# VectorE's convolution lane moved from two units ahead to one, and the second block's dense convolution cut to one group

## The chip, the cores and the metric

The kernel runs on one core of a Trainium2 chip. The metric is the device time of one launch in microseconds (us); of the runs shown, the median counts. TensorE (PE in the profile) does the matmuls, VectorE (DVE), ScalarE (ACT) and GpSimd (POOL) the elementwise work, and SyncE (SP) issues transfers. Each has its own queue of instructions. Matmul results go to PSUM, which here is handed out in four tiles of two banks each.

## The reference

A causal convolution over 7 tokens, whose weights are a softmax per head (8 heads of 24 columns), is followed by a gated feed-forward layer with ReLU. There are 8 batches of 4096 tokens and 192 columns; the hidden width is 1536.

```python
w = np.exp(weight - np.max(weight, axis=-1, keepdims=True))
w = w / (np.sum(w, axis=-1, keepdims=True) + 1e-09)
x_pad = np.concatenate([np.zeros((B, pad, D)), x], axis=1)
idx = np.arange(S)[:, None] + np.arange(K)[None, :]
x_unf = x_pad[:, idx, :].reshape(B, S, K, H, group)
a = np.einsum('hk,bskhg->bshg', w, x_unf).reshape(B * S, D)
gate = np.maximum(a @ w_gate, 0.0)
val = a @ w_val
return gate * val @ w_out
```

## The kernel before

**Units and streams.** The work is cut into 16 units of 1024 tokens (`UNIT`). Each is done for two streams at once (`st`): batch b and batch b + 4. The convolved input of a unit is the tile `xc[u]`: partitions 0 to 63 hold one stream and 64 to 127 the other, with the 192 columns in three chunks (`c`), and the tokens run along the free dimension.

**The main loop** (lines 648 to 685) does for each unit u: the gates (`gate_val`, twice, for 512 tokens each), then the projection (`project`). In `gate_val`, each of 12 steps f makes 12 matmuls (line 505) into two PSUM tiles, one for the gate and one for the value; ScalarE takes the ReLU of the first (line 516), VectorE multiplies it by the second (line 517) into `hT`. A PSUM tile is free again when its reader is done.

**The projection** multiplies `hT` by `Wo` for four halves (512 tokens of one stream each). In units 1 to 15 `half_pass` does it with matmuls of 64 rows (line 536), in two turns for a half, the turns of different halves interleaved: (0,0), (1,0), (0,1), (2,0), (1,1), (3,0), (2,1), (3,1), as (half, turn). The second turn of a half writes the same banks from other rows, so it must wait for the first turn to end. That wait goes by way of SyncE: an empty instruction in SyncE's queue (line 549) waits for the last matmul of the first turn, and the first matmul of the second turn waits for it (line 546). In unit 0 `half_whole` does it with full 128-row matmuls (line 556) and no such wait. `evict` (line 573) copies a half's result to SBUF, and SyncE issues the write to DRAM (line 574).

**The convolution** has two ways.

- *Dense, on TensorE*, for units 0 and 1. `GROUPS` lists four groups of five token pieces. Groups 0 and 1 make unit 0: `conv_dense`, one call for each chunk of columns (line 333), with one PSUM tile each. Group 0 stands before the gates, and the three calls of group 1 stand in unit 0's first gates, ahead of f = 5, 7 and 9. Groups 2 and 3 make unit 1: `conv(g, part)`, eight matmuls (line 358) in two parts with one PSUM tile each. ScalarE moves the results in five copies to a tile `y` (line 373), and SyncE issues one transposing transfer for each token piece from `y` into `xc[1]` (line 395). Group 2 stands after unit 0's gates, group 3 after the first half of its projection.
- *The lane*, for units 2 to 15, two units ahead: while unit u runs, the lane makes unit u + 2. GpSimd issues four loads of x into `x_e` (`lane_load`, line 414), copies them into another order in `x_p` (line 433), and SyncE issues nine transposing transfers (line 436) into `x_r`. The first 576 tokens (`LDVE`) are VectorE's: ScalarE makes the first products (`lane_first`, line 469), VectorE adds 18 shifted products (`lane_rest`, line 481). The other 448 tokens (`LPOOL`) are GpSimd's: ScalarE (line 452) and VectorE (line 454, the list `VECTOR`) make products into `prods`, and GpSimd adds them (line 458) during the gates of the next unit.

**Order.** The schedule is manual: each engine's queue holds its instructions in the order in which the program text makes them. After unit u's gates come `lane_first` and `lane_rest` of unit u + 2 and then `project(u)`, in which ScalarE's products and the copies of the results alternate.

**The head.** GpSimd loads the gate and value weights in column pieces (`load_w`) into partitions 0 to 63, and `both_halves` copies each piece into partitions 64 to 127: VectorE does pieces 0 and 1, GpSimd (`pool_halves`, line 180) the others. Piece 3 serves f = 5 and 6, piece 4 f = 7 and 8, piece 5 f = 9 to 11. After these copies GpSimd issues the loads for lane 2 and for groups 2 and 3 and the load of `Wo`.

Of the kernel before, what the change touches and what calls it, by code (L numbers as in the profile page):

```python
# [15 lines left out]
def kernel(  # L16
# [26 lines left out]
    VECTOR = [  # L43
        [(0, 5), (1, 5), (2, 5), (0, 4), (1, 4), (2, 4), (2, 1)],
        [(0, 5), (1, 5), (2, 5), (0, 6), (2, 1)],
    ]
# [11 lines left out]
    second = [min(t, 2 * UNIT - SUB) for t in range(UNIT, 2 * UNIT, SUB)]  # L58
    GROUPS += [(0, second[:GSUB]), (0, second[GSUB:])]
# [3 lines left out]
    xpool = ctx.enter_context(tc.tile_pool(name="xpool", bufs=3))  # L63
# [3 lines left out]
    ypool = ctx.enter_context(tc.tile_pool(name="ypool", bufs=2))  # L67
# [7 lines left out]
    def load_x(g):  # L75


        bp, toks = GROUPS[g]
        xt = xpool.tile([128, GSUB, 2, D], F16, name="x_h")
        rows, step = (SUB, DSUB) if g < 2 else (128, SUB)  # L80
        for st in range(2):
            b = bp + NB * st
            last = toks[-1] - toks[-2] != step
            n_full = len(toks) - int(last)
            src = bass.AP(
                tensor=x.tensor,
                offset=x.offset + (b * S + toks[0] - PAD) * D,
                ap=[[D, rows], [step * D, n_full], [1, D]],
            )
            nc.gpsimd.dma_start(out=xt[0:rows, 0:n_full, st, :], in_=src)  # L90
            if last:
                nc.gpsimd.dma_start(
                    out=xt[0 : SUB + PAD, len(toks) - 1, st, :],
                    in_=x[b, toks[-1] - PAD : toks[-1] + SUB, :],
                )
        return xt

# [87 lines left out]

    load_w(0)
# [5 lines left out]
    load_w(4, 6)  # L192
    pool_halves(3)

# [150 lines left out]
    convs = {}  # L345

    def conv(g, part):


        xt = xts[g]  # L350
        bp, toks = GROUPS[g]
        n = len(toks)
        rows = SUB + PAD
        W = 2 * n * G
        ps = psum.tile([128, 2, 512], FP, name="ps")
        for h, (t, bank, slot) in PLACE.items():
            if t == part:
                nc.tensor.matmul(  # L358
                    out=ps[0:SUB, bank, W * slot : W * (slot + 1)],
                    lhsT=band(h),  # L360
                    rhs=xt[0:rows, 0:n, :, G * h : G * (h + 1)],
                    start=True,
                    stop=True,
                    skip_group_check=True,
                )
        if part == 0:
            convs[g] = ypool.tile([128, GSUB, NCH, 2, 64], F16, name="y")
        y = convs[g]

        def move(copy, bank, i0, step_in, c, r0, step_out, width):  # L370
            src = ps[0:SUB, bank, 0 : 2 * W]
            dst = y[0:SUB, 0:n, 0, :, 0:1]
            copy(
                out=bass.AP(
                    tensor=dst.tensor,
                    offset=dst.offset + 128 * c + r0,
                    ap=[dst.ap[0], [step_out, 2], [NCH * 128, n], [64, 2], [1, width]],
                ),
                in_=bass.AP(
                    tensor=src.tensor,  # L380
                    offset=src.offset + i0,
                    ap=[src.ap[0], [W + step_in, 2], [2 * G, n], [G, 2], [1, width]],
                ),
            )

        if part == 0:
            move(nc.scalar.copy, 0, 0, 0, 0, 0, G, G)
            move(nc.scalar.copy, 1, 0, 0, 1, 8, G, G)
            return
        move(nc.scalar.copy, 0, 0, 0, 2, 16, G, G)  # L390
        move(nc.scalar.copy, 1, 0, 8, 0, 48, 2 * 128 - 48, 16)
        move(nc.scalar.copy, 1, 16, -16, 1, 0, 56, 8)
# [7 lines left out]
    xes, xrs, accs, prods = {}, {}, {}, {}  # L400

    def lane_load(u):


        bp, t0 = u * UNIT // S, u * UNIT % S
        xe = epool.tile([128, TILES, 2, NCH, 64], F16, name="x_e")
        j0 = int(t0 == 0)
        if j0:
            nc.gpsimd.memset(xe[0:HALO, 0, :, :, :], 0.0)
        for st in range(2):  # L410
            b = bp + NB * st
            for j, n in ((j0, TDVE - j0), (TDVE, TILES - TDVE)):
                lo = t0 - HALO + 128 * j if j < TDVE else t0 + LDVE - HALO
                nc.gpsimd.dma_start(  # L414
                    out=xe[:, j : j + n, st, :, :].rearrange("p j c r -> p j (c r)"),
                    in_=bass.AP(
                        tensor=x.tensor,
                        offset=x.offset + (b * S + lo) * D,
                        ap=[[D, 128], [128 * D, n], [1, D]],
                    ),  # L420
                )
            if j0:
                nc.gpsimd.dma_start(
                    out=xe[HALO:128, 0, st, :, :].rearrange("p c r -> p (c r)"),
                    in_=x[b, 0 : 128 - HALO, :],
                )
        xes[u] = xe

    def lane_turn(u):
        xe = xes.pop(u)  # L430
        xp = epool.tile([128, TILES, NCH, 2, 64], F16, name="x_p")
        for st in range(2):
            nc.gpsimd.tensor_copy(out=xp[:, :, :, st, :], in_=xe[:, :, st, :, :])  # L433
        xr = rpool.tile([128, NCH, 128 * TILES], F16, name="x_r")
        for j in range(TILES):
            nc.sync.dma_start_transpose(
                out=xr[:, :, 128 * j : 128 * j + 128],
                in_=xp[:, j].rearrange("p c s r -> p (c s r)"),
            )
        xrs[u] = xr  # L440

    def shifted(u, c, k, lane):
        o = HALO - KW + 1 + k
        if lane:
            return xrs[u][:, c, 128 * TDVE + o : 128 * TDVE + o + LPOOL]
        return xrs[u][:, c, o : o + LDVE]

    def product(engine, u, c, k):
        out = prods[u][:, k, c, :]
        in_, scale = shifted(u, c, k, 1), tap[:, c, k : k + 1]  # L450
# [5 lines left out]
    def add(u, k):  # L456
        pr = prods[u]
        nc.gpsimd.tensor_tensor(  # L458
            out=pr[:, 0] if k < KW - 1 else xc[u][:, :, LDVE:UNIT],
# [5 lines left out]
    def lane_first(u):  # L465
        accs[u] = apool.tile([128, NCH, LDVE], FP, name="acc")
        xc[u] = xcpool.tile([128, NCH, UNIT], F16, name="xc")
        for c in range(NCH):
            nc.scalar.activation(  # L469
                out=accs[u][:, c, :],  # L470
                in_=shifted(u, c, 0, 0),
# [3 lines left out]
        prods[u] = apool.tile([128, KW, NCH, LPOOL], FP, name="prods")  # L475

    def lane_rest(u):
        acc = accs.pop(u)
        for k in range(1, KW):
            for c in range(NCH):  # L480
                nc.vector.scalar_tensor_tensor(  # L481
                    out=xc[u][:, c, 0:LDVE] if k == KW - 1 else acc[:, c, :],
                    in0=shifted(u, c, k, 0),
# [5 lines left out]
        for c, k in VECTOR[u > 2]:  # L489
            product(nc.vector, u, c, k)  # L490

    def gate_val(u, w):
        h = hpool.tile([128, NFF, 2, WIN], F16, name="hT")
        xcb = xc[u]
        for f in range(NFF):
            if u == 0 and w == 0 and f in (5, 7, 9):
                conv_dense(1, (f - 5) // 2)
# [28 lines left out]
    SYNC = mybir.DependencyInfo(mybir.DependencyClass.Sync, mybir.DependencyReason.DATA)  # L526

# [24 lines left out]

    def half_whole(h, st, outs):
        for q in range(4):
            for f in range(NFF):
                nc.tensor.matmul(  # L556
                    out=outs[q],
                    lhsT=h[:, f, st, 128 * q : 128 * (q + 1)],
                    rhs=Wo[:, f, :],
                    start=(f == 0),  # L560
                    stop=(f == NFF - 1),
                )
# [45 lines left out]
    def project(u, hs, work):  # L608
# [3 lines left out]
        if u == 0:  # L612
            order = [(i, 2) for i in range(4)]
        if u == NUNIT - 1:
            order = [(0, 0), (1, 0), (0, 1), (2, 0), (1, 1), (2, 1), (3, 2)]
        for i, turn in order:
# [5 lines left out]
            if turn in (0, 2):  # L622
                at[i] = slots()
            if turn in (1, 2):
                for c, k in work[i]:
                    product(nc.scalar, u + 2, c, k)
            if turn == 2:
                half_whole(h, st, at[i][1])
            else:
                done[i] = half_pass(h, st, at[i][1], turn, done.get(i))  # L630
            if turn:
                evict(at[i][0], row0, u > 0 and i == 3 or u == NUNIT - 1 and i == 2)
            if u == 0 and i == 0:
                conv(3, 0)
                conv(3, 1)
# [7 lines left out]
    pool_halves(5)  # L643
    nc.gpsimd.tensor_copy(out=tap[64:128], in_=tap[0:64])
    lane_load(2)
    xts[2] = load_x(2)
    nc.gpsimd.dma_start(out=Wo[:], in_=moe_w_out.rearrange("(c p) d -> p c d", p=128))
    for u in range(NUNIT):
        lane = 1 <= u < NUNIT - 1
        if lane:  # L650
            add(u + 1, 1)
        if u == 1:
            lane_load(3)
            add(2, 2)
            add(2, 3)
# [3 lines left out]
        if u + 2 < NUNIT:  # L659
            lane_turn(u + 2)  # L660
        if u == 0:
            xts[3] = load_x(3)
# [53 lines left out]
```

## Time and profile before

| what | value |
|---|---|
| median of 3 runs | 768.06 us (767.74 to 768.5) |
| the profiled execution's own time | 767.88 us |
| its span in the profile | 765.9 us |
| ReLU, line 516 | 386 times, mean 1019 ns |
| gate product, line 517 | 386 times, mean 1215 ns |
| product and sum on VectorE, line 481 | 210 + 42 times, mean 811 and 810 ns |
| product on ScalarE, line 452 | 222 times, mean 662 ns |
| product on VectorE, line 454 | 72 times, mean 446 ns |
| addition on GpSimd, line 458 | 70 + 14 times, mean 3034 and 3027 ns |
| transposing transfer, line 395 | 10 times, 1174 / 1246 / 1814 ns (least, median, most) |
| transposing transfer, line 436 | 126 times, 1180 / 1257 / 3183 ns |
| load of x_e, line 414, issue to landing | 4.2 / 6.1 / 9.5 us |
| empty instruction, line 549 | 59 times, 17 ns each |

How to read it: the page gives the busy time of each engine and its share of the span. The chain that ended last is followed back from the last instruction, at each step to what released it; "PE ps L505" is TensorE's work of line 505 into the tile `ps`. Lines of a timeline have start, length, engine, line, operation, output<-inputs, shape and count; a bracket gives the idle time before and what ended it. "SPq" and "POOL DMA" lines are the issuing of transfers, not the moving of the data. The gaps between instructions of one engine can be smaller than the durations suggest, since the next one starts before the end of the last is reported.

### The profile page before, as it was taken

To read this page: it belongs to the slowest core of one execution; us is meant where nothing else is said; L and a number is where in the kernel's file an instruction comes from. 1 tells how busy PE (TensorE), PEld (TensorE's weight loads), DVE (VectorE), ACT (ScalarE), POOL (GpSimd) and SP (SyncE) were. 2 spreads that over 40 slices of the span, in tenths; PEclk is the share of its full clock that TensorE was granted. 3 is DMA by queue.
4 is the path that set the end of the run, shared out by engine and by line. 5 is a ranking of instruction groups with operands and counts; after the bars stand their busy time and mean duration, and the time that the engine had idled before them with its cause. 6 is when DMAs were issued, how large, how long until landed. Compare 5 with 4: busy or idle time off the path is not lost.

```text
span 765.9 us, 24782 instructions
## 1 busy us (share of the span) xinstructions
PE 761.7 (99%) x10794; PEld 502.5 (66%) x10794; DVE 692.7 (90%) x746; ACT 600.7 (78%) x735; POOL 369.9 (48%) x212
## 2 busy tenths in 40 slices
PE   9999999999999999999999999999999999999998
PEld 4595674946749476584755848567484674947648
DVE  7999999999999999999999999999999999996591
ACT  6797887878878787887878878788787887875571
POOL 8608648093570926619166290743908346090000
PEclk9999999999999999999999999999999999999999
DMA  8966727190472804528054281722919131200202
GB/s 121 134 104 116 92 91 88 54 122 6 100 78 66 110 23 97 61 85 95 23 111 47 85 92 44 106 31 85 93 44 117 21 92 39 65 22 15 71 2 84
DMA packets 131810, 56.12 MB, mean 73 GB/s; under 512 B 96741, under 2 KB 131701, under 8 KB 131701
## 3 DMA queue, kind: packets, MB, share of 16 engines
q1 hardware_dynamic: 90789, 38.85, 25.1%
q0 software_dynamic: 40768, 15.59, 18.9%
q8 instruction: 84, 1.38, 0.8%
q14 instruction: 25, 0.20, 0.1%
q10 hardware_dynamic: 144, 0.10, 0.0%
HBM read 31.68 MB, written 25.17 MB: 74 GB/s over the span
## 4 chain that ended last, share of the span: by engine, by line
PE 99%; DMA 1%; issue 0%; POOL 0%; ACT 0%; POOLq 0%
PE ps L505 65%; PE ps L536 31%; PE ps L556 2%; DMA x_h<-in_x_dram 1%; PE ps L594 1%; PE ps L333 0%; PE ps L358 0%; POOL spaced L129 0%; ACT acc L573 0%; POOLq L700 0%
## 5 line engine op out<-in xcount | busy, mean ns | idle before, releaser
L517 DVE TENSOR_TENSOR hT<-gr,ps 128x1024 f16<-128x1024 f16 (+1 forms) x386 | 468.9, 1215 | 37.0 <-ACT gr L516 9.9
L516 ACT ACTIVATE gr<-ps 128x1024 f16<-128x1024 f32 (+1 forms) x386 | 392.9, 1019 | 102.4 <-PE ps L505 100.6
L458 POOL TENSOR_TENSOR prods<-prods 128x1344 f32<-128x1344 f32 x70 | 212.4, 3034 | 309.1 <-DVE prods L454 305.7
L505 PE MATMUL ps<-xc,Wg 64*128 64x512 f16 x2304 | 311.9, 376 | 0.0
L505 PE MATMUL ps<-xc,Wv 64*128 64x512 f16 x2304 | 311.8, 376 | 0.0
L536 PEld LDWEIGHTS <-hT 64*128 64x128 f16 x5664 | 234.1, 94 | 3.6
L536 PE MATMUL ps<-Wo,hT 64*128 64x192 f16 x5664 | 236.1, 243 | 0.0
L505 PEld LDWEIGHTS <-Wv 64*128 64x128 f16 x2304 | 129.8, 94 | 118.5 <-DVE hT L517 0.3
L505 PEld LDWEIGHTS <-Wg 64*128 64x128 f16 x2304 | 112.2, 94 | 132.4 <-issue 0.2
L481 DVE SCALAR_TENSOR_TENSOR acc<-x_r,tap,acc 128x576 f32<-128x576 f16 x210 | 154.3, 811 | 1.6 <-ACT acc L469 1.6
L452 ACT ACTIVATE prods<-x_r,tap 128x448 f32<-128x448 f16 x222 | 130.3, 662 | 0.0
L573 ACT COPY out_s<-ps 128x768 f32<-128x768 f32 (+1 forms) x63 | 45.7, 725 | 52.4 <-PE ps L536 42.5
L414 POOL DMA_DIRECT2D x_e<-in_x_dram x56 | 45.1, 818 | 3.4 <-POOL x_p L433 3.4
L433 POOL COPY x_p<-x_e 128x1728 f16<-128x1728 f16 x28 | 44.7, 1624 | 1.7 <-DMA x_e<-in_x_dram 1.6
L458 POOL TENSOR_TENSOR xc<-prods 128x1344 f16<-128x1344 f32 x14 | 42.4, 3027 | 1.1
L481 DVE SCALAR_TENSOR_TENSOR xc<-x_r,tap,acc 128x576 f16<-128x576 f16 x42 | 31.8, 810 | 0.0
L573 DVE COPY out_s<-ps 128x384 f32<-128x384 f32 x15 | 8.3, 550 | 25.5 <-ACT out_s L573 25.5
L469 ACT ACTIVATE acc<-x_r,tap 128x576 f32<-128x576 f16 x42 | 29.4, 766 | 0.0
L454 DVE TENSOR_SCALAR prods<-x_r,tap 128x448 f32<-128x448 f16 x72 | 27.3, 446 | 0.0
L556 PE MATMUL ps<-Wo,hT 128*128 128x192 f16 x192 | 16.2, 246 | 0.0
L556 PEld LDWEIGHTS <-hT 128*128 128x128 f16 x192 | 15.9, 98 | 0.0
L90 POOL DMA_DIRECT2D x_h<-in_x_dram x6 | 4.9, 825 | 0.0
(54 smaller groups left out, 66.9 us busy)
## 6 DMA issues: line engine op xcount, KB each, us to landing
out_dram<-out_s SPq DMA_DIRECT2D x63, 384.0 KB
x_e<-in_x_dram POOLq DMA_DIRECT2D x34, 192.0 KB, 6.2
x_e<-in_x_dram POOLq DMA_DIRECT2D x22, 240.0 KB, 4.8
x_r<-x_p SPq DMA_TRANSPOSE x126
Wo<-in_moe_w_out_dram POOLq DMA_DIRECT2D x1, 576.0 KB
x_h<-in_x_dram POOLq DMA_DIRECT2D x2, 240.0 KB, 7.6
x_h<-in_x_dram POOLq DMA_DIRECT2D x2, 210.0 KB, 5.1
x_h<-in_x_dram POOLq DMA_DIRECT2D x2, 192.0 KB, 7.6
```

The source lines that it names most:

```text
L414: nc.gpsimd.dma_start(out=xe[:, j : j + n, st, :, :].rearrange("p j c r -> p j (c r)"), in_=bass.AP(tensor=x.tensor, offset=x.offset + (b ...
L433: nc.gpsimd.tensor_copy(out=xp[:, :, :, st, :], in_=xe[:, :, st, :, :])
L452: engine.activation(out=out, in_=in_, func=ACTF.Copy, scale=scale)
L458: nc.gpsimd.tensor_tensor(out=pr[:, 0] if k < KW - 1 else xc[u][:, :, LDVE:UNIT], in0=pr[:, 0], in1=pr[:, k], op=ALU.add,)
L469: nc.scalar.activation(out=accs[u][:, c, :], in_=shifted(u, c, 0, 0), func=ACTF.Copy, scale=tap[:, c, 0:1],)
L481: nc.vector.scalar_tensor_tensor(out=xc[u][:, c, 0:LDVE] if k == KW - 1 else acc[:, c, :], in0=shifted(u, c, k, 0), scalar=tap[:, c, k : k ...
L505: nc.tensor.matmul(out=pss[i][:, st, :], lhsT=W[64 * st : 64 * st + 64, c, 128 * f : 128 * (f + 1)], rhs=xcb[64 * st : 64 * st + 64, c, WI ...
L516: nc.scalar.activation(out=gr[:, sts], in_=pss[0][:, sts], func=ACTF.Relu)
L517: nc.vector.tensor_tensor(out=h[:, f, sts], in0=gr[:, sts], in1=pss[1][:, sts], op=ALU.mult)
L536: mm = nc.tensor.matmul(out=outs[q], lhsT=h[64 * r : 64 * r + 64, f, st, 128 * q : 128 * (q + 1)], rhs=Wo[64 * r : 64 * r + 64, f, :], sta ...
L556: nc.tensor.matmul(out=outs[q], lhsT=h[:, f, st, 128 * q : 128 * (q + 1)], rhs=Wo[:, f, :], start=(f == 0), stop=(f == NFF - 1),)
L573: one(out=dst[:, step * j : step * j + step], in_=src[:, step * j : step * j + step])
```

## The change

VectorE's part of the lane is now made one unit ahead and GpSimd's part two units ahead. Lane v (v = 1 to 15) makes the first 576 tokens of unit v and the last 448 tokens of unit v + 1; `pieces(v)` gives the two pieces of x. While unit u runs, lane u + 1 is made. Lane 15 has no GpSimd part.

- Of unit 1, only the last 448 tokens are convolved on TensorE: one group of four pieces, `GROUPS[2]`, in place of groups 2 and 3. `conv` fills two PSUM tiles at once, and `conv_out` holds ScalarE's five moves and SyncE's transposing transfers. `conv` stands after unit 0's gates, and `lane_first(1)` now stands between it and `conv_out`.
- The three calls of `conv_dense` for group 1 stand together ahead of f = 6.
- `half_whole` is gone: unit 0's projection uses `half_pass` in the same order as the other units, and its last result is split between ScalarE and VectorE as theirs are.
- Lane 1's x is loaded at the head, through the generator `lane_load`: two loads ahead of `pool_halves(3)`, one behind it, the last after `pool_halves(5)`. Its turn comes in two halves, with the load of `Wo` and of group 2 between them. Lane 2's load is held until `lane_first(1)` is done (`hold`).
- `lane_turn` makes four copies of parts in place of two of the whole.
- `VECTOR` is one list of five products; before, unit 2's lane had seven. In lane 1, GpSimd makes two products itself (`FOR_POOL`). All of a lane's additions on GpSimd now stand ahead of the unit's gates in the program text.
- `xpool` has two buffers in place of three, `ypool` one in place of two.

```diff
-    VECTOR = [
-        [(0, 5), (1, 5), (2, 5), (0, 4), (1, 4), (2, 4), (2, 1)],
-        [(0, 5), (1, 5), (2, 5), (0, 6), (2, 1)],
-    ]
+    VECTOR = [(0, 5), (1, 5), (2, 5), (0, 6), (2, 1)]
+    FOR_POOL = [(1, 6), (2, 6)]
...
-    second = [min(t, 2 * UNIT - SUB) for t in range(UNIT, 2 * UNIT, SUB)]
-    GROUPS += [(0, second[:GSUB]), (0, second[GSUB:])]
+    GROUPS += [(0, list(range(UNIT + LDVE, 2 * UNIT, SUB)))]
...
+    def pieces(v):
+        both = [(0, TDVE, v * UNIT)]
+        if v + 1 < NUNIT:
+            both.append((TDVE, TILES - TDVE, (v + 1) * UNIT + LDVE))
+        return both
+
+    def lane_load(v, hold=None):
...
+                if hold is not None:
+                    tc.add_manual_dep(first.ins, hold.ins.name, SYNC, reason="behind the turns of the lane before")
+                    hold = None
...
+    ahead = lane_load(1)
+    next(ahead)
+    next(ahead)
     pool_halves(3)
+    next(ahead)
...
-    def conv(g, part):
+    def conv(g):
...
+        wide = [psum.tile([128, 2, 512], FP, name="ps") for _ in range(2)]
+        for h, (t, bank, slot) in PLACE.items():
+            nc.tensor.matmul(
+                out=wide[t][0:SUB, bank, W * slot : W * (slot + 1)],
...
+        return wide
+
+    def conv_out(g, wide):
...
+        y = ypool.tile([128, GSUB, NCH, 2, 64], F16, name="y")
...
+        move(nc.scalar.copy, 0, 0, 0, 0, 0, 0, G, G)
+        move(nc.scalar.copy, 0, 1, 0, 0, 1, 8, G, G)
+        move(nc.scalar.copy, 1, 0, 0, 0, 2, 16, G, G)
+        move(nc.scalar.copy, 1, 1, 0, 8, 0, 48, 2 * 128 - 48, 16)
+        move(nc.scalar.copy, 1, 1, 16, -16, 1, 0, 56, 8)
         for jj, t in enumerate(toks):
             u, k = t // UNIT, min(SUB, UNIT - t % UNIT)
             nc.sync.dma_start_transpose(
...
+    def lane_turn(v):
...
+        for j0, n, _ in pieces(v):
+            for st in range(2):
+                nc.gpsimd.tensor_copy(
+                    out=xp[:, j0 : j0 + n, :, st, :], in_=xe[:, j0 : j0 + n, st, :, :]
                 )
+            for j in range(j0, j0 + n):
+                nc.sync.dma_start_transpose(
...
-            if u == 0 and w == 0 and f in (5, 7, 9):
-                conv_dense(1, (f - 5) // 2)
+            if u == 0 and w == 0 and f == 6:
+                for c in range(NCH):
+                    conv_dense(1, c)
...
-        if u == 0:
-            order = [(i, 2) for i in range(4)]
...
-                evict(at[i][0], row0, u > 0 and i == 3 or u == NUNIT - 1 and i == 2)
-            if u == 0 and i == 0:
-                conv(3, 0)
-                conv(3, 1)
+                evict(at[i][0], row0, i == 3 or u == NUNIT - 1 and i == 2)
...
     pool_halves(4)
     pool_halves(5)
+    load_rest(ahead)
     nc.gpsimd.tensor_copy(out=tap[64:128], in_=tap[0:64])
-    lane_load(2)
+    between = lane_turn(1)
+    next(between)
+    nc.gpsimd.dma_start(out=Wo[:], in_=moe_w_out.rearrange("(c p) d -> p c d", p=128))
     xts[2] = load_x(2)
-    nc.gpsimd.dma_start(out=Wo[:], in_=moe_w_out.rearrange("(c p) d -> p c d", p=128))
+    load_rest(between)
     for u in range(NUNIT):
...
+        adds = 1 <= u < NUNIT - 1
+        if u + 1 < NUNIT:
+            xc[u + 1] = xcpool.tile([128, NCH, UNIT], F16, name="xc")
+        if adds:
+            add(u, 1)
         hs = []
         if u == 0:
             hs.append(gate_val(0, 0))
...
+        if 0 < u < NUNIT - 1:
+            load_rest(lane_turn(u + 1))
+        if 0 < u < NUNIT - 2:
+            load_rest(lane_load(u + 2))
+        if u == 1:
+            for c, k in FOR_POOL:
+                product(nc.gpsimd, u, c, k)
+        if adds:
+            for k in range(2, KW):
+                add(u, k)
         while len(hs) < 2:
             hs.append(gate_val(u, len(hs)))
...
+        wide = conv(2) if u == 0 else None
+        if u + 1 < NUNIT:
+            last = lane_first(u + 1)
+            if u == 0:
+                conv_out(2, wide)
+                load_rest(lane_load(2, last))
+            lane_rest(u + 1)
         if u + 2 < NUNIT:
...
         project(u, hs, work)
```

## The prediction

> **What bounds the kernel now.** I read the page first (busy shares, the chain that ended last), then that chain in order of time, then the timeline of each engine around the places that the change touches.
>
> ```profile
> PE 761.7 (99%) x10794; PEld 502.5 (66%) x10794; DVE 692.7 (90%) x746; ACT 600.7 (78%) x735; POOL 369.9 (48%) x212
> PE 99%; DMA 1%; issue 0%; POOL 0%; ACT 0%; POOLq 0%
> ```
>
> TensorE is the chain. A gain must take matmuls, or a wait, out of its row, and any new wait in that row is paid in full. The chain in order of time shows the stretch that the change rewrites, and then one ordinary unit:
>
> ```profile
> 21.57 19.56 PE ps L505 x180
> 41.13 0.99 PE ps L358 x8
> 42.12 3.96 PE ps L556 x48
> 46.09 0.82 PE ps L358 x8
> 46.91 11.88 PE ps L556 x144
> 58.79 31.19 PE ps L505 x288
> 89.97 15.84 PE ps L536 x384
> ```
>
> Unit 0's gates end at 41.13 and unit 1's start at 58.79: 17.66 us, in which two dense convolutions (0.99 and 0.82) stand among 15.84 of whole projections. A later unit takes 46.92 us (31.08 gates, 15.84 projection), with no hole.
>
> **What leaves TensorE's row.** Of the two groups only group 2 stays, now of 4 pieces instead of 5 (192 columns a matmul, not 240). Its second tile is still the one that VectorE frees with the last but one gate product (about 41.5), so I take 0.95 for it, between 0.8 x 0.99 = 0.8 and 0.99. The 192 whole matmuls become 384 half ones; 48 + 144 of the former took 15.84, 384 of the latter take 15.84: nothing. So 17.66 becomes 0.95 + 15.84 = 16.79: **-0.9**, if nothing waits.
>
> Group 1's three pieces (40 matmuls, 0.56 each) move together ahead of f = 6. Around each one the 24 gate matmuls take 2.70 where 288 in 31.08 make 2.59, so 0.11 a switch, and two switches go: **-0.2**. They take three of the four PSUM tiles, so f = 6 begins with the tile that VectorE's product of f = 5 frees. I work that out as 17.95, against 17.87 for TensorE: **+0.1**.
>
> **What is moved in GpSimd's queue at the head.** Two of lane 1's loads now stand ahead of the copy of the weights' upper halves for f = 5.
>
> ```profile
> 11.54 0.63 POOL L173 DMA_DIRECT2D Wv<-in_moe_w_val_dram  x1
> 13.17 0.82 POOL L180 COPY Wg<-Wg 64x768 f16<-64x768 f16 x1 [1.01 <-DMA Wg<-in_moe_w_gate_dram]
> 13.94 0.83 POOL L180 COPY Wv<-Wv 64x768 f16<-64x768 f16 x1
> 19.72 3.30 POOL L414 DMA_DIRECT2D x_e<-in_x_dram  x4
> ```
>
> Four such issues take 3.30, so two take 1.63: from 12.18 to 13.81. The wait of 1.01 hides part; the Wg copy ends near 14.63 instead of 13.99, Wv near 15.41. Before, a dense piece filled 14.41 to 14.98; now f = 5 wants its upper half at 14.43 and 15.37. With 0.1 for the signal that is 0.30 + 0.14: **+0.4**; bounds 0 (signal and copy earlier) and 0.9. The third load puts the halves for f = 7 at 17.9 and the last at 20.2, against wants of 19.2 and 21.8: nothing. Lane 1's copies then start at 21.2, its nine transposes at about 1.4 us (12.87 for nine) end near 36, and ScalarE asks for them at 41.4.
>
> **The new wait: SyncE's queue in unit 0.** Half passes come in two turns. The second turn of a half waits for an empty SyncE instruction (line 549) that waits for the first turn. Unit 0 used none before: the 59 in the trace are four in each later unit, less one. Now it has four, and in SyncE's queue they stand behind conv_out's four transposes, which wait for ScalarE's five moves, which now stand behind lane_first.
>
> ```profile
> 40.52 1.02 ACT L516 ACTIVATE gr<-ps 128x1024 f16<-128x1024 f32 x1 [0.27 <-PE ps L505]
> 41.71 2.00 ACT L373 CAST y<-ps 112x480 f16<-112x480 f32 x5 [0.17 <-PE ps L358]
> 43.57 2.14 ACT L469 ACTIVATE acc<-x_r,tap 128x576 f32<-128x576 f16 x3
> 47.82 0.81 ACT L573 COPY out_s<-ps 128x768 f32<-128x768 f32 x1
> 43.74 6.92 SPq L395 DMA_TRANSPOSE xc<-y  x5
> 50.76 0.53 SPq L574 DMA_DIRECT2D out_dram<-out_s  x1
> 51.39 8.21 SPq L395 DMA_TRANSPOSE xc<-y  x5
> 59.71 1.86 SPq L574 DMA_DIRECT2D out_dram<-out_s  x3
> ```
>
> The last four lines show what a queue behind transposes costs: the first output is in SBUF at 48.63, and its write starts at 50.76, right after the fifth transpose. Two more outputs are copied by 56.4 and their writes start at 59.71, after the next five.
>
> The new order from these rows: ReLU from 40.52, lane_first from 41.44 (0.92 later, as 370.89 to 371.81 in the seventh projection) to 43.53, moves from 43.45. Five moves of 1920 elements took 2.00; 384 fewer at 0.83 ns (1024 elements in 1.02 us against 384 in 0.48) leave 1.68: y complete at 45.13. The transposes start 0.03 later. Single ones run 1.17 to 1.81 us, median 1.25; the first four of group 2 took from 43.74 to 49.40 with the gaps, 5.66, and four median ones would take 5.2. I take 5.5: SyncE is free at 50.7, TensorE has its signal at 50.85. It wants it after conv and two half passes: 41.02 + 0.95 + 3.96 = 45.9. **TensorE stands idle for 4.9 us.** Bounds: 4.5 with the median ones; 6.7 if each takes the longest of group 2, 1.81, since lane 2's x now loads in this stretch. What is next in that queue (the write of the first output, the later turns' signals) comes due only after TensorE has moved on, at intervals of 2 us, so one stall and not four.
>
> [...]
>
> **What is hidden.** Lane 1 adds 18 products-and-sums (13.2 us, as 373.08 to 386.30) to VectorE's total, but they take lane 2's old place in unit 0; what is really added is lane 15 in unit 14's projection, where VectorE sat idle for 14.77 us. Uncovered, it would be 13 us. The price of one unit less lead is a deadline: xc must be ready when the next unit's gates start.
>
> ```profile
> 384.03 2.27 DVE L481 SCALAR_TENSOR_TENSOR xc<-x_r,tap,acc 128x576 f16<-128x576 f16 x3
> 387.17 0.81 PE L505 MATMUL ps<-xc,Wg 64*128 64x512 f16 x6
> ```
>
> It ends at 386.30 and is wanted at 387.17: 0.87 to spare, within 0.02 at all thirteen such boundaries, so nothing. In unit 0 the stall itself gives more. GpSimd's two products in unit 1 are not shown: between the 0.45 us of VectorE's product and the 3.03 of an addition of three times the elements. I take 1.0, nearest to a third of the addition. Even at 3.03 each its additions end near 89, and the buffer is overwritten from about 96. Four x_p copies for two add at most 2 x 0.2 (the smallest copy) to a queue that idles 21.7 us a unit. The load of lane 2, held to 43.5, lands by 46.8 + 9.5 = 56.3, and is copied after 61. Unit 0's last output, now split between ScalarE and VectorE, is as in every other unit.
>
> **Sum.** -0.9 - 0.2 + 0.1 + 0.4 + 4.9 = +4.3. The profiled execution took 767.88 (765.9 of span and 1.98 around it), 0.18 below the median of 768.06; 772.2 and 772.4, so **772.3**. From unit 1 on nothing changes.
>
> **The rivals.** *Forecast*, chance 0.48: 772.3, own range 771.3 to 774.1 by the bounds.
>
> *The idle stretch slows the matmuls after it*, 0.30. The trace's only matmuls after a long idle are the first:
>
> ```profile
> 0.86 2.83 PE L157 MATMUL ps<-const-bfloat16-1.0 128*128 128x512 bf16 x7 [0.86 <-PEq L700]
> ```
>
> 3200 columns in 2.83 us are 1.13 a ns, against 288 x 512 / 2 in 31.08, 2.37 a ns, later. A 512 wide one takes 0.61 still at 4.09 and 0.38 at 5.15, so the slow stretch is 3.2 to 4.3 long and costs half of itself, 1.8: 774.1. Against it: no idle of this length follows matmuls anywhere in this trace, and the granted clock shows full speed throughout. [...]
>
> *SyncE does not hold TensorE*, 0.10: the place is the first second turn, at 45.9; it decides if the four transposes leave the queue within 0.75 us, 0.19 each, where the rows have 1.25, or if the signal goes ahead of them. Then -0.9 - 0.2 + 0.1 + 0.4 = -0.6: 767.5, not slower.
>
> *VectorE misses the deadline*, 0.06: at all 15 boundaries TensorE pays what exceeds 0.87; 0.3 over would add 4.5, 776.8. For it: one late row would do it fifteen times. Against it: the same rows at thirteen boundaries. The last 0.06 is for what I have not seen.
>
> **Range and chances.** 770.8 to 775.3 holds the first two cases; the third, the fourth and the remainder leave out under 2 in 10. No change means within 0.2% (1.5 us), about what a measurement of this kernel can tell. Slower: 0.48 + 0.30 + 0.06 and 0.02 of the rest, 0.86. Within: 0.08 of the third and 0.01, 0.09. Faster: 0.02 and 0.03, 0.05.
>
> **What would show it.** In the profile after: one hole of about 5 us in TensorE's row, after the first 96 half matmuls of unit 0's projection, released by SyncE; in SyncE's queue four transposes from about 45 and the first empty instruction near 51; unit 1's gates near 63; from there 46.92 a unit. Half-rate matmuls after the hole speak for the second case, no hole for the third, a hole at each unit's first gate with VectorE as releaser for the fourth. The f = 5 gates should show 0.4 of waiting on GpSimd. I am wrong if the time is below 770, or if the hole has another releaser.

## The result

The changed kernel takes 775.65 us (median of 5, 775.48 to 775.69), the kernel before 768.39 in the same comparison: ratio 1.0096, 95% interval 1.0081 to 1.0111. It is 7.3 us slower, where 4.3 were forecast, and 0.35 above the range. The profiled execution took 775.69, with a span of 773.7. In the table of experiments, one of e10's twelve executions took 1345.67 us at a granted clock of 0.655; its ratio leaves that one out.

First the page after the change: busy times, and the chain that ended last, by engine and by line.

```profile
PE 763.9 (99%) x10978; PEld 500.5 (65%) x10978; DVE 705.6 (91%) x763; ACT 600.9 (78%) x733; POOL 377.3 (49%) x242
PEclk9989999999999999999999999999999999999999
PE 96%; POOL 1%; DMA 1%; SPq 1%; issue 1%; ACT 0%; POOLq 0%; ACTq 0%
```

TensorE is busy for 2.2 us more than before although a dense group is gone, the chain has 4% outside of it, and the granted clock, always 9 before, has an 8 in the third slice (38 to 58 us). The chain in order of time, from unit 0's gates on:

```profile
19.04 1.16 POOL Wv L171
20.20 0.65 issue
20.85 21.59 PE ps L517 x198
...
45.48 1.58 ACT y L410 x5
47.07 1.18 SPq L430
48.29 1.25 SPq L430
49.58 1.31 SPq L430
50.94 1.25 SPq L430
...
52.31 14.33 PE ps L546 x288
66.64 31.08 PE ps L517 x288
97.72 15.84 PE ps L546 x353
```

The four transposes are on the chain, and the six half passes behind them take 14.33 us where eight take 15.84 in unit 1. Another piece reads differently: "issue" at 20.20 is time in which TensorE waited for nothing that the profile shows. The chain puts a copy that ended at 20.20 ahead of it; e6 below shows that TensorE did not need that copy. From TensorE's starts in the timelines:

| stage | before | after | difference |
|---|---|---|---|
| start to unit 0's first gate | 7.80 | 8.16 | +0.36 |
| first gate to the projection's first matmul | 34.16 | 35.76 | +1.60 |
| projection to unit 1's first gate | 16.76 | 22.55 | +5.79 |
| unit 1's first gate to the end | 707.15 | 707.21 | +0.06 |

Everything happens in the first 67 us. Of the +5.79, one dense group less gives -0.9 (16.76 holds 0.9 for group 3); the idle stretch and slow matmuls make the rest. In the timeline (start, length, idle before and what ended it):

```profile
42.46 1.02 ACT L528 ACTIVATE gr<-ps 128x1024 f16<-128x1024 f32 x1 [0.27 <-PE ps L517]
43.38 2.10 ACT L478 ACTIVATE acc<-x_r,tap 128x576 f32<-128x576 f16 x3
43.92 4.13 PE L546 MATMUL ps<-Wo,hT 64*128 64x192 f16 x96
45.38 1.67 ACT L410 CAST y<-ps 112x384 f16<-112x384 f32 x5
47.07 5.12 SPq L430 DMA_TRANSPOSE xc<-y  x4
52.31 14.33 PE L546 MATMUL ps<-Wo,hT 64*128 64x192 f16 x288 [4.25 <-SPq L559]
66.47 0.81 PE L517 MATMUL ps<-xc,Wg 64*128 64x512 f16 x6
```

ReLU, lane_first, moves, transposes, signal: each starts as the one before it ends, and TensorE starts 4.4 us after the 47.88 (43.92 + 3.96) at which it could have. From 52.31 to 66.47 it needs 14.16 for six half passes, against 6/8 of 15.84 = 11.88: 2.3 lost. The table by stretches shows why; its columns are the stretch, its length, busy time of PE, PEld, DVE, ACT and POOL (with the number of instructions), granted clock, share of the DMA engines, GB/s. The share adds up the times of all packets, so it can be above 1.

```profile
44.00:47.90 3.90, 3.90 (x96) 3.82 (x96) 3.90 (x6) 3.90 (x10) 1.88 (x3) 1.00 0.14 7
47.90:52.30 4.40, 0.15 (x4) 0.00 (x0) 4.40 (x7) 1.94 (x4) 1.31 (x2) 0.76 1.33 156
52.30:54.00 1.70, 1.69 (x22) 1.59 (x24) 1.70 (x3) 0.00 (x0) 0.00 (x0) 0.50 1.54 167
54.00:56.00 2.00, 2.00 (x30) 1.86 (x28) 2.00 (x4) 0.00 (x0) 0.00 (x0) 0.50 0.77 125
56.00:58.00 2.00, 2.00 (x42) 1.93 (x38) 2.00 (x4) 1.63 (x3) 0.00 (x0) 0.74 0.03 8
58.00:60.00 2.00, 2.00 (x54) 2.00 (x50) 1.68 (x5) 1.97 (x4) 0.17 (x1) 1.00 0.65 197
```

The clock falls to 0.50 at 50.22, during the idle stretch, and stays there until 57.04 by the profile's clock record: 4.7 us of matmuls at half rate lose 2.4, near the 2.3 measured. The +1.60 ahead of the projection is mostly a hole ahead of f = 7:

```profile
17.18 0.84 POOL L171 COPY Wv<-Wv 64x768 f16<-64x768 f16 x1
18.84 0.83 PE L517 MATMUL ps<-xc,Wv 64*128 64x512 f16 x6
20.85 0.33 PEld L517 LDWEIGHTS <-Wg 64*128 64x128 f16 x6 [1.68 <-issue]
```

f = 7 should start 0.645 after 18.84, at 19.49; it starts at 20.85, 1.4 late. Its weights, piece 4, were copied by 18.02; the copies of piece 5 behind them ended at 20.20.

### The profile page after: what moved, and what is told of

It reads as the page before. It is cut to its first block, busy times and chain, and to the rows that moved or that the text cites. A ratio compares the mean times of both kernels' runs of the same rounds, so it can differ in the third digit from the quotient of the medians.

```text
span 773.7 us, 25194 instructions
## 1 busy us (share of the span) xinstructions
PE 763.9 (99%) x10978; PEld 500.5 (65%) x10978; DVE 705.6 (91%) x763; ACT 600.9 (78%) x733; POOL 377.3 (49%) x242
## 4 chain that ended last, share of the span: by engine, by line
PE 96%; POOL 1%; DMA 1%; SPq 1%; issue 1%; ACT 0%; POOLq 0%; ACTq 0%
PE ps L517 63%; PE ps L546 32%; DMA Wg<-in_moe_w_gate_dram 1%; SPq L430 1%; PE ps L593 1%; POOL Wg L171 0%; POOL Wv L171 0%; POOL Wv L164 0%; POOL Wg L164 0%; POOL x_h L84 0%; ACT y L410 0%; ACT acc L478 0%; POOL x_e L197 0%; POOL spaced L122 0%; POOL spaced L120 0%
## 5 line engine op out<-in xcount | busy, mean ns | idle before, releaser
L546 PE MATMUL ps<-Wo,hT 64*128 64x192 f16 x6048 | 254.5, 244 | 4.3 <-SPq L559 4.3
L546 PEld LDWEIGHTS <-hT 64*128 64x128 f16 x6048 | 251.7, 95 | 8.5 <-SPq L559 4.5
L490 DVE SCALAR_TENSOR_TENSOR acc<-x_r,tap,acc 128x576 f32<-128x576 f16 x225 | 165.3, 812 | 0.0
L197 POOL DMA_DIRECT2D x_e<-in_x_dram x58 | 46.9, 817 | 22.2 <-ACT acc L478 18.9
L442 POOL COPY x_p<-x_e 128x960 f16<-128x960 f16 (+1 forms) x58 | 50.4, 910 | 0.1
L490 DVE SCALAR_TENSOR_TENSOR xc<-x_r,tap,acc 128x576 f16<-128x576 f16 x45 | 34.1, 812 | 0.0
L478 ACT ACTIVATE acc<-x_r,tap 128x576 f32<-128x576 f16 x45 | 31.4, 764 | 0.0
L148 PE MATMUL ps<-const-bfloat16-1.0 128*128 128x512 bf16 (+1 forms) x10 | 4.2, 560 | 0.9 <-PEq L691 0.9
L380 ACT CAST xc<-ps 128x512 f16<-128x512 f32 x4 | 2.3, 586 | 2.4 <-PE ps L370 2.4
L593 PE MATMUL ps<-Wo,hT 128*128 128x192 f16 x48 | 4.1, 246 | 0.0
```

Of the source, the lines that this page charges most:

```text
L197: first = nc.gpsimd.dma_start(out=xe[:, j0 + start : j0 + n, st, :, :].rearrange("p j c r -> p j (c r)"), in_=bass.AP(tensor=x.tensor, off ...
L442: nc.gpsimd.tensor_copy(out=xp[:, j0 : j0 + n, :, st, :], in_=xe[:, j0 : j0 + n, st, :, :])
L478: last = nc.scalar.activation(out=accs[v][:, c, :], in_=shifted(v, c, 0, 0), func=ACTF.Copy, scale=tap[:, c, 0:1],)
L490: nc.vector.scalar_tensor_tensor(out=xc[v][:, c, 0:LDVE] if k == KW - 1 else acc[:, c, :], in0=shifted(v, c, k, 0), scalar=tap[:, c, k : k ...
L546: mm = nc.tensor.matmul(out=outs[q], lhsT=h[64 * r : 64 * r + 64, f, st, 128 * q : 128 * (q + 1)], rhs=Wo[64 * r : 64 * r + 64, f, :], sta ...
```

## The experiments

They compare the three losses: the idle stretch (4.4), the slow matmuls (2.3), the hole (1.4). Since the head differs between executions (first gate from 7.42 to 8.91 over fourteen profiles, with the same instructions ahead of it), the verdicts rest on the stages within each profile.

| run | first gate to projection | projection to unit 1 | median, us | ratio to before (interval) |
|---|---|---|---|---|
| before, and once more | 34.16, 34.29 | 16.76, 16.76 | 768.0 to 768.4; once more, one run: 767.72 | |
| after | 35.76 | 22.55 | 775.65 | 1.0096 (1.0081 to 1.0111) |
| e1 signals first | 36.79 | 16.91 | 770.69 | 1.0035 (1.0021 to 1.0048) |
| e2 wait filled | 37.25 | 20.53 | 774.16 | 1.0073 (1.0060 to 1.0086) |
| e3 moves first | 37.33 | 20.54 | 775.10 | 1.0087 (1.0070 to 1.0105) |
| e4 whole matmuls | 35.71 | 15.94 | 769.50 | 1.0014 (1.0005 to 1.0023) |
| e5 pieces spread | 34.83 | 23.11 | 773.77 | 1.0082 (1.0068 to 1.0096) |
| e6 loads late | 34.88 | 22.73 | 774.56 | 1.0086 (1.0073 to 1.0099) |
| e7 = e1 and e5 | 34.26 | 16.17 | 768.07 | 0.9999 (0.9990 to 1.0007) |
| e9 = e4 and e5 | 34.63 | 15.94 | 767.16 | 0.9989 (0.9980 to 0.9997) |
| e10 = e9, loads late | 34.13 | 15.93 | 767.46 | 0.9995 (0.9986 to 1.0004) |
| e11 = e7, no hold | 34.25 | 15.85 | 767.42 | 0.9991 (0.9982 to 0.9999) |
| e12 short idle | 38.74 | 19.51 | 774.92 (one run) | |

**e1: the signals ahead of the transposes.** The lane's part of unit 0 is written behind the first two half passes:

```diff
+            if n == 2 and between is not None:
+                between()
...
-        project(u, hs, work)
+        project(u, hs, work, lane_part if u == 0 else None)
```

> Only the order of unit 0 is changed: its first two half passes are written ahead of the lane's part, so the two empty SyncE instructions stand ahead of the four transposes. Theory (the signals wait behind the transposes, and the idle stretch lowers the matmul clock): the idle 4.43 and the slow 2.28 both go, 775.65 - 6.7 = 768.9. Rival A (TensorE waits for the transposes' data or for ScalarE's moves, not for the queue): the idle stays, 775.6. Rival B (the slow half passes come from the x loads and transposes that run at the same time, not from the idle): only the idle goes, 771.2 with half passes still slow after 52.

The idle stretch and the slow matmuls are both gone: 16.91 from projection to gates instead of 22.55, with the transposes still running from 48.75 to 53.86. So SyncE's order made the wait, not the transposes' data nor ScalarE. Rival A falls, and rival B too, since x's packets are in the same stretch (DMA share 1.57 and 1.61 from 50 to 54, at a granted clock of 1.00). The 1.8 us by which 770.69 misses 768.9 are the head of these executions (36.79, of which f = 5 takes more than in after) and a new hole of 0.88 in the projection, both taken up below.

```profile
44.45 12.55 PE L546 MATMUL ps<-Wo,hT 64*128 64x192 f16 x299
57.88 3.71 PE L546 MATMUL ps<-Wo,hT 64*128 64x192 f16 x85 [0.88 <-issue]
```

**e2: the wait filled.** The order of after, with TensorE kept busy while it waits:

```diff
+            if u == 0 and (i, turn) == (0, 1):
+                for _ in range(76):
+                    nc.tensor.matmul(
+                        out=at[1][0][:, 1, 2 * D : 512],
+                        lhsT=busy[:, 0:128],
+                        rhs=busy[:, 0:128],
...
```

> 76 matmuls of 128 columns, whose results nobody reads, fill TensorE's wait in unit 0's projection; the wait itself stays. Theory (idle lowers the clock): no slow stretch, 775.65 - 2.28 = 773.4, and the granted clock is 1.00 from 48 to 58. Rival B (transfers slow the matmuls): the half passes after the wait stay slow, 775.6. If the filling runs longer than the wait, up to 0.3 more.

Its timeline shows the filling (line 621) and the six half passes after it:

```profile
48.80 4.65 PE L621 MATMUL ps<-const-bfloat16-1.0 128*128 128x128 bf16 x76
53.38 12.05 PE L546 MATMUL ps<-Wo,hT 64*128 64x192 f16 x288
```

12.05 instead of 14.33, granted clock 1.00 in every stretch from 44 to 60, and x's packets at the same time (DMA share 1.47 at 52 to 54). So it was the idle stretch that lowered the clock, and these transfers did not slow the matmuls. The stage is 2.0 shorter, not 2.28, since the second turn starts 8.64 after the projection's first matmul, 0.25 later than in after (8.39). The rest of the distance from 773.4 to 774.16 is in the head (37.25).

**e3: ScalarE's moves ahead of lane 1's first products.**

```diff
+            if u == 0:
+                conv_out(2, wide)
             last = lane_first(u + 1)
             if u == 0:
-                conv_out(2, wide)
                 load_rest(lane_load(2, last))
```

> ScalarE's five moves stand ahead of lane 1's three first products again, so the transposes start some 1.8 us earlier and the wait is about 2.6 us instead of 4.43. [...] If any idle stretch lowers the clock: 775.65 - 1.8 = 773.8. If the transposes do not set the wait: 775.6.

TensorE is idle for 2.86 us and the clock still drops: it stands at 0.67, 0.50 and 0.93 in the three stretches from 52.3 to 58, and the six half passes take 13.54 from 52.22 to unit 1's gates, 1.7 lost. The expectation of a drop (773.8) holds for the stage (-2.0); in the total the head of these executions took most of it back (37.33; the runs of e3 lie between 773.28 and 778.48).

**e12: the same with a shorter wait.** As e3, with 26 of the filling matmuls.

> As e3 (moves first, idle 2.86 us, and 1.66 lost to slow matmuls after it), with 26 matmuls that nobody reads ahead of the wait, which leave about 1.4 us idle. If a drop needs a longer idle stretch, the granted clock stays 1.00 after the wait and nothing is lost but the idle; if any stretch does it, another 1.7 is lost.

After 1.45 us of idle the clock stays at 1.00. But the same execution shows a drop at another place, behind the hole of f = 7 (here 19.09 to 21.42):

```profile
19.10:21.40 2.30, 0.36 (x4) 0.00 (x0) 1.22 (x1) 0.77 (x1) 2.24 (x4) 1.00 0.41 49
21.40:22.50 1.10, 1.08 (x10) 0.50 (x12) 0.00 (x0) 0.22 (x1) 1.10 (x2) 1.00 0.98 93
22.50:24.00 1.50, 1.50 (x10) 0.56 (x8) 0.66 (x1) 0.80 (x1) 1.50 (x3) 0.54 0.58 72
24.00:26.00 2.00, 2.00 (x12) 0.77 (x10) 0.85 (x2) 1.02 (x1) 2.00 (x3) 0.50 0.84 91
```

The gates run at half rate from about 22.5 to 26. So idle stretches of 4.4 and 2.9 us lowered the clock, and one of 1.96 (the hole here) did too, while 1.45 did not, nor did the 2.19 of the same hole in e2, where the clock is 1.00 throughout. The length alone does not decide it near 2 us. The clock records of the five traces with a drop have a pattern. Counted from the first rise to full clock, every change falls within 0.01 us of a whole multiple of 3.413 us:

```text
run    full clock from   at half rate      multiples of 3.413   TensorE idle in the 3.41 us before the drop
after   5.84             50.22 to 57.04    13 and 15            2.16
e3      5.10             52.88 to 56.30    14 and 15            2.75
e5     10.28             51.24 to 58.06    12 and 14            3.37
e6      4.50             48.87 to 55.70    13 and 15            2.39
e12     5.54             22.61 to 26.02    5 and 6              1.96
```

Idle is here the time without a matmul in the profile. On the same grid, the most of it in a stretch that was not followed by a drop, over all fourteen profiles, is 1.53 (e3, from 18.75 to 22.16). The 2.19 of e2 lie across an edge of its grid, at 20.63, so that the two stretches hold 1.28 and 1.04. The full clock came back after a stretch in which matmuls ran throughout, in all five; one with 0.85 of idle (e5, from 51.24 to 54.65) did not bring it back. All this fits a drop after 1.96 us or more of idle in one stretch of the grid, and none after 1.53 or less. That it is the share of one stretch which counts is the author's estimate from this table; no run was made to test it.

**e4: whole matmuls again in unit 0.** `half_whole` and its order are back; everything else is as after.

> Unit 0's projection made of whole matmuls again, as before the change; everything else as after. Theory: no signals, so no idle and no drop, 775.65 - 6.7 = 768.9, the same as with the signals first, since 192 whole and 384 half matmuls both take 15.84. If half passes are faster or slower in unit 0 for another reason, the two differ.

15.94 in the stage: no signals, no idle, no drop. Eight half passes of a later unit take 15.84 (97.55 to 113.39 in after), so whole and half matmuls cost the same here, as costed. The hole of f = 7 is still there (19.12 to 20.84). It outweighs the dense group that is gone: from the first gate to unit 1's first gate e4 takes 51.66, the kernel before 50.92 and 51.05.

**e5: the dense pieces spread again; e6: lane 1's loads late.** Each undoes one of the two edits at the head:

```diff
-            if u == 0 and w == 0 and f == 6:
-                for c in range(NCH):
-                    conv_dense(1, c)
+            if u == 0 and w == 0 and f in (5, 7, 9):
+                conv_dense(1, (f - 5) // 2)
```
```diff
     ahead = lane_load(1)
-    next(ahead)
-    next(ahead)
     pool_halves(3)
-    next(ahead)
```

> Group 1's three dense pieces go back to f = 5, 7 and 9; unit 0's projection stays as after, with its wait. The question is TensorE's hole of 1.4 us ahead of f = 7 (19.29 to 20.85 in the profile after), whose weights were copied at 18.03. Theory I (TensorE ran out of instructions: 240 of them went in 1.5 us, and the next block of 16 KB was fetched at 18.59 behind x's packets): the hole goes, and the wait of f = 5 with it, about 1.5 earlier in unit 0's last gates. Theory P (the weights' copies, moved behind x's loads in GpSimd's queue, come too late): a hole stays ahead of f = 7 or f = 5.

> All four loads of lane 1 behind the last copy of the weights; the dense pieces stay together ahead of f = 6. Theory I: the hole ahead of f = 7 shrinks or goes only as far as the fetch of instructions is no longer behind x's packets; the burst of 240 is still there, so some may stay. Theory P: no hole at f = 7 and none at f = 5. In both, lane 1 is still ready in time, and the wait in the projection stays.

The hole ahead of f = 7 is gone in both, and it is in all five profiles that have both edits (after, e1, e2, e3, e4) and in e12. So neither edit makes it alone. e5's stage is 0.93 shorter than after's, not the 1.5 expected, since in this execution its first gates take 0.65 longer than in before (7.26 against 6.61 up to the first dense piece). The packets of queue q8, of the kind "instruction" in the profile, show how the two edits meet. It moves 16 KB at a time: 84 packets before, where TensorE has 21,605 instructions (matmuls and weight loads), and 86 after, where it has 21,968, so 257 and 255 for each. Three blocks in a row of after start when 2,498, 2,754 and 3,010 have started, 256 apart. That they are TensorE's instructions is inferred from these numbers. Here is the second block of each profile, with the number of instructions that TensorE had started by then:

```text
run            second block fetched   started by then   hole ahead of f = 7
before         15.50 to 16.48         511               none
before again   15.18 to 16.07         507               none
after          18.59 to 19.54         691               19.29 to 20.85
e1             19.06 to 19.95         695               19.57 to 21.38
e4             18.14 to 19.17         687               19.12 to 20.84
e5 (spread)    18.40 to 19.29         531               none
e6 (late)      16.59 to 17.57         493               none
e9 (spread)    18.45 to 19.41         589               none
e10 (both)     15.41 to 16.30         493               none
```

Counted from the start of TensorE's 505th instruction, the block starts from 0.4 us before it to 0.3 after it in the four profiles with late or no loads of lane 1 at the head (before, again, e6, e10), and 1.4 to 3.0 after it in the ten with early ones. Where it is late the DMA engines are busy: from 17.0 to 18.6 their share is 1.48 in after and 1.54 in e5, 0.00 in before and e6. How x's packets hold the block up is not shown. With the three pieces together TensorE starts 240 instructions in 1.5 us, and the hole begins each time after instruction 705. e1's second hole begins after instruction 1729, which is 705 and four blocks of 256; there half passes, 96 instructions in 1.98 us, ran while lane 2's x was loaded. None of the semaphores that f = 7's first matmuls wait for changed between 20.2 and 20.85 in the profile after, and the weights were there at 18.02. The copy that ended at 20.20 is not what f = 7 waited for: in e6 f = 7 starts at 19.29, before that copy ends (19.82). So theory P falls. Theory I fits all of these numbers; that TensorE had no instructions left is inferred from them, since no row of the profile names it.

What stays in e6 is the wait of f = 5: with no dense piece in front of it, its weights' upper half comes late by themselves (the Wg copy waits 1.76 for its load). In the profiles with early loads this wait varies a good deal: from the first matmul of f = 5 to the first dense piece, 1.39 without a wait (f = 6 in before), it takes 1.56 in e4, 1.68 in after, 2.22 in e2, 2.23 in e12, 2.58 in e1 and 3.21 in e3. With the hole of f = 7 (1.4 to 2.4) and e12's slow gates, this makes the differences between their heads in the table.

**e7, e9, e10, e11: what the change is worth without its costs.** e7 joins e1 and e5; e9 joins e4 and e5; e10 adds the late loads to e9; e11 is e7 with `lane_load(2)` in place of `lane_load(2, last)`.

> Signals first (as in e1) and the dense pieces spread (as in e5). If the account by stages is right, what is left of the change is one dense group less: 0.9 under the kernel before, 767.5, and 0.9 more than that where TensorE runs out of instructions in the projection as it did at 57.0 in e1.

> Whole matmuls in unit 0's projection (as e4) and spread dense pieces (as e5): neither signals nor a burst of instructions. Theory: what is left is one dense group less, so unit 1's gates start 0.9 earlier after the first gates than in the kernel before (50.15 instead of 51.05 from first gate to first gate), and the time is 768.0 - 0.9 = 767.1, faster by 0.1%. Rival (the deadline of the shorter lead, or the lane's own work, costs something that the stall has hidden): 768.0 or more, with holes at the units' first gates.

> As e9, and lane 1's loads behind the weights' copies. If early loads only delay the fetch of instructions, and that is covered once the pieces are spread, this equals e9 within 0.2; if they still cost the head something, it is faster by that, 766.8 or so; if lane 1 comes late to ScalarE, slower.

> As e7 (half passes, signals first, dense pieces spread), but lane 2's loads are not held until lane 1's first products are done, so their packets go at about 28 us and not during unit 0's projection. Theory (x's packets delay the fetch of instructions, and half passes use them up twice as fast as whole ones): the block that was fetched at 1620 instructions in e7 is fetched near 1470 again, no hole of 0.14 at 54.5, project to gates 15.9 instead of 16.17. If the holes of e1 and e7 come from elsewhere, no change.

From first gate to unit 1's first gate before took 50.92 and 51.05; e9 takes 50.57, e10 50.06, e11 50.10: up to 0.9 is there, as costed for one dense group. In e9 part of it goes into waits of f = 5; in the totals e10 does not show its shorter head (767.46 against 767.16). e9 and e11 are the only versions whose interval lies below 1, and only just: 767.16 and 767.42 against 767.97, 0.1% faster. The profiled executions of e7 and e11 end 0.6 and 0.8 later behind unit 1's first gate (707.72 and 707.99 against 707.15), behind the issue of the last write, so their stages gain more than their times. In e7 the block that is fetched near 1470 instructions elsewhere (1465 before) was fetched at 1620, with a hole of 0.14; in e11, without lane 2's packets in that stretch, at 1468, with no hole and 15.85 instead of 16.17 (DMA share from 50 to 52: 1.57 in e7, 0.25 in e11). That bears out the cause of e1's second hole.

**The kernel before, once more.**

> The kernel before, once more, for its head: in the two profiles shown unit 0's first gates start at 7.80 and, after the change, 8.16, with the same instructions ahead of them. If that is a difference between executions, this one may differ from 7.80 as much; if the change makes it, it is 7.80 again within 0.05.

7.51 instead of 7.80: the start of the first gate differs by 0.3 between executions of one program. The +0.36 of the stage table is of that size and is not laid to the change.

## Why the prediction was wrong, point by point

- **The wait behind the transposes** was right in place, order and releaser. Its size was 4.4, not 4.9: the four transposes took 5.12, below the 5.5 taken, and the dense convolution with four pieces was no shorter than the one with five (0.92 from its first matmul to the projection's, 0.90 before), where 0.04 less was taken. e1 and e4 show that it is the signals.
- **The third case**, that SyncE does not hold TensorE, fell: it needed the four transposes out of the queue within 0.75 us, and they held SyncE for 5.12, up to 52.19; TensorE went on at 52.31.
- **The slow matmuls after the idle** are the term that was put wrong: it stood as the second case with 0.30, the author's own judgement, and it came in after, in e3, e5 and e6. Its price was 1.8 and it measured 2.3, since the slow stretch was 4.7 long and not 3.2 to 4.3. By the table at e12 no stretch of the grid was idle as a whole (2.16 of 3.41 us in after), and 4.25 us of idle (the bracket in the timeline) leave at least 2.1 in one stretch wherever the edges fall, above the 1.96 that sufficed in e12. Sum of the forecast with the measured wait and this term: -0.9 - 0.2 + 0.1 + 0.4 + 4.4 + 2.3 = 6.1. A shorter idle stretch sufficed too: 2.86 us in e3, and 1.96 in e12.
- **"The third load puts the halves for f = 7 at 17.9 ... nothing"** is the step that failed outright. The halves were there, at 18.02 against 19.49 wanted. But the same two edits, early loads and pieces together, made a hole of 1.4 us ahead of f = 7, by the account at e6 for want of instructions. The burst was costed by the PSUM tiles that it takes, the loads by GpSimd's time, and neither by what they do to the fetch. 6.1 + 1.4 = 7.5, where the medians differ by 7.3. With 6.1 alone the time would have been 774.2, inside the range; the hole took it out.
- **The rest of the head** was near: f = 5 lost 0.3 (0.4 forecast), which is partly luck, since the same wait cost up to 1.8 in e3; the pieces together took 1.66 up to f = 6 instead of 2.01 (three times 0.56 and the 0.11 of a switch), so -0.35 (-0.1 forecast for both terms).
- **The deadline of the shorter lead** held. The unit after unit 1, in the timeline of after:

```profile
110.25 2.27 DVE L490 SCALAR_TENSOR_TENSOR xc<-x_r,tap,acc 128x576 f16<-128x576 f16 x3
113.39 0.81 PE L517 MATMUL ps<-xc,Wg 64*128 64x512 f16 x6
```

  It ends at 112.52 and is wanted at 113.39, 0.87 as before, and a unit takes 46.92 at each of the 14 steps from unit 1 to unit 15. The fourth case fell; VectorE's 18 more products and sums are hidden, as costed.
- **What was hidden elsewhere** stayed hidden: GpSimd's two products in unit 1 took 2.83 together (2.0 taken, bounds 0.9 and 6.1).

## What to carry to other kernels

The wait that went through SyncE's queue cost what stood ahead of it there (4.4 us behind four transposes), so each new user of such a signal (here one projection made like the others) needs the whole queue read from its place back. The idle stretch on TensorE was paid again in the matmuls behind it (2.3 us after 4.25 of idle, 1.7 after 2.86 in e3), and cheap matmuls that nobody reads took that second payment away (six half passes in 12.05 us in e2, 14.33 in after). Where many short matmuls stand together, look at what the DMA engines carry at that time: with x's loads beside it, the second block of instructions started 1.4 to 3.0 us after TensorE's 505th instruction, against 0.3 at most without.

## What had not been expected of the hardware

- TensorE stopped after instructions 705 and 1729, for 1.3 to 2.4 us beyond the regular step at the first, when the block was fetched some 180 instructions later than in the kernel before (691 in after, 511 before); it started again 1.3 to 1.7 us after the fetch was over (after, e1, e4). That it had run out of instructions is inferred. The stop stands in the profile as idle "<-issue" (1.68 in after) or is laid to a product of VectorE ("<-DVE hT", 2.19 in e2, 1.96 in e12).
- The clock fell to 0.50 after 2.86 us of idle, and once after 1.96, and stayed there for 3.4 or 6.8 us; after 1.45 us, and once after 2.19, it did not fall. In the five traces with a drop its changes lie on a grid of 3.413 us. It fell after a stretch of the grid with 1.96 or more of idle, and not after one with 1.53 or less in any of the fourteen profiles.
- Four transposes of 112 tokens hold SyncE for 5.1 to 5.8 us in eleven profiles of the changed program, in which x's loads run beside them, at least in part. In e11, where the loads come earlier, it was 6.25, since one of the four took 2.42.
